# A decode-attention kernel: the value step turned round (keys' values stream past fixed probabilities) and the branch sum spread over four column groups

## The chip, the cores and the metric

The kernel runs on one core of one Trainium2 chip. The metric is device time in microseconds (us), the median over several executions of the same program. Two executions of this kernel are rarely more than 0.4% apart (192.45 to 193.17 us over eight).

In the text, PE is the matrix engine (TensorE), PEld its weight loads, DVE the vector engine, ACT the scalar engine, POOL GpSimd and SP the engine that issues most transfers. A matmul has a fixed operand, loaded as weights, and a moving operand, which streams past it column by column. "Granted clock" is the share of PE's full clock that the chip's throttle let through, as the profile shows it.

## The reference, cut to what matters

One token for each of two batch rows goes through attention over a cached window of 4096 keys, beside a dense branch; both are added to the input.

```python
# B=2, Sq=1, D=448; 16 query heads, 8 key/value heads (rep=2), head size 256
W = min(4096, max(256, Sk // 4))                  # 4096
q = (xn @ wq) split into 16 heads of 256
k = k_cache[:, :, Sk - W:, :]; v = v_cache[:, :, Sk - W:, :]   # each kv head serves 2 query heads
scores = einsum("bhqd,bhkd->bhqk", q, k) * 256 ** -0.5
p = softmax(scores)
o = einsum("bhqk,bhkd->bhqd", p, v)
attention = o.reshape(B, 1, 16 * 256) @ wo        # 4096 -> 448
h = xn @ w1 + b1                                  # 448 -> 1792
dense = (h * tanh(softplus(h))) @ w2              # 1792 -> 448
out = x + attention + dense                       # (2, 1, 448), bf16
```

All inputs are bf16. Keys and values are 2 MB per (key/value head, batch row), 16 such pairs of each, and with the weights some 78 MB have to be read.

## The kernel before, in words

The kernel works through 16 "heads" `i` (a key/value head and a batch row; `b = 1` at odd `i`). Everything is issued in the order written, on every engine (`issue_in_order`).

For each head there are two halves `s = 2i` and `2i + 1`, of 16 blocks of 128 keys each:

- `turn(s)` (L356): DVE transposes the half's keys in 32x32 blocks, once the 2 MB of keys have landed.
- `scores(s)` (L368): eight matmuls of 512 columns with the spread-out query (`qdiag`, built by POOL in `build_q`, L249) as weights. ACT takes the exponential (L378) and, with it, the row sums.
- `turn_p(s)` (L389): DVE transposes the probabilities. After the second half it forms the sums (L396, L399), PE adds them over partitions (`den`, L403), and DVE takes the reciprocal `rec` (L405).
- `values(i)` (L415): 64 matmuls. Each loads 128x128 of the values as weights and moves 2 columns (the two query heads' probabilities) past them. The result, 128 partitions x 2 halves of the head size x 2 query heads, lies in `po`, of which there are two in turn. DVE multiplies it by `rec` into `oT` (L426).
- `mix(kvh)` (L206, by the helper `add`): after each second head, eight matmuls with two columns of `oT` (both batch rows) as weights and 224 columns of `wo` moving, added into `psA`, one tile of two rows for each half of the 448 output columns.

The main loop (L457) goes over `i = 0..17`. In turn `i` it issues the loads of keys `i+2` and values `i`; then for each half `turn(s+1)`, `scores(s)`, `turn_p(s-1)`; and at the end `values(i-2)` and, at odd heads, `mix`. Turn 16 has only the last `turn_p`, `values(14)`; turn 17 `values(15)` and the last `mix`. At the end (L487, L488) DVE and ACT each copy one half of the sum to `res`, and SP sends it out.

All big loads go through SP's queue, in order: keys into four buffers, values into five (shared with `wq`, `w1`, `w2`), `wo` into three. So the load of values `i` waits for `values(i-5)` to be done with its buffer. The last head's values come in three pieces, and the last `wo` in two.

The dense branch is done in the first two turns: `dense_in` (L275) and `dense_out`, whose 28 matmuls go through `add` as well.

Of the kernel before, what the change touches and what calls it, by code (L numbers as in the profile page):

```python
# [9 lines left out]
ALU = mybir.AluOpType  # L10
AXIS = mybir.AxisListType
BF16 = mybir.dt.bfloat16
FP32 = mybir.dt.float32
PSUM = bass.MemoryType.PSUM
# [20 lines left out]
def kernel(  # L35
# [13 lines left out]
    nc = tc.nc  # L49
    P = 128  # L50
    Q = 32
    NQ = P // Q

    Bsz, Sq, D = A_x.shape
    _, Hkv, Sk, Dh = A_k_cache.shape
    HqDh = A_wq.shape[1]
    Hq = HqDh // Dh
    rep = Hq // Hkv
# [3 lines left out]
    T = W // P  # L62
    NH = 2
    TH = T // NH
# [6 lines left out]
    ND = Dh // P  # L71
    NB = Dh // (2 * Q)
    NE = 2
    assert Sq == 1 and D * NX == NS * P and NS % 2 == 1 and HF % P == 0 and Hq % NX == 0
    assert TH * Q <= 512 and NB * NE * Q == Dh and ND == 2
    scale = float(Dh) ** -0.5
# [3 lines left out]
    ident = lead.tile([P, P], BF16)  # L80
    hsel = lead.tile([P, Q], FP32)
# [4 lines left out]
    consts = ctx.enter_context(tc.tile_pool(name="consts", bufs=1))  # L86
    p_pool = ctx.enter_context(tc.tile_pool(name="pp", bufs=3))
    small = ctx.enter_context(tc.tile_pool(name="small", bufs=3))
    ps_sc = ctx.enter_context(tc.tile_pool(name="ps_sc", bufs=2, space=PSUM))
    ps_o = ctx.enter_context(tc.tile_pool(name="ps_o", bufs=2, space=PSUM))  # L90
    ps_den = ctx.enter_context(tc.tile_pool(name="ps_den", bufs=1, space=PSUM))
    ps_a = ctx.enter_context(tc.tile_pool(name="ps_a", bufs=1, space=PSUM))
    ps_m = ctx.enter_context(tc.tile_pool(name="ps_m", bufs=1, space=PSUM))
# [2 lines left out]
    x_bf = consts.tile([Bsz, D], BF16)  # L96
# [14 lines left out]
    for lo, hi in ((0, SC), (SC, NS)):  # L111
        w = v_tile((hi - lo) * HW).rearrange("p (s n) -> p s n", n=HW)
# [2 lines left out]


    make_identity(nc, ident[:])
    eps_t = consts.tile([Bsz, 1], FP32)
    nc.vector.memset(eps_t[:], 1e-5)

# [7 lines left out]
        out=rstd[:], in_=mv[:, 1:2], func=ACT.Sqrt, bias=eps_t[:], scale=1.0  # L128
# [5 lines left out]
    for r in range(2):  # L134
        n = (NS + 1 - r) // 2
        nc.vector.tensor_scalar(  # L136
            out=xn_bf[:, r : NS : 2, :, :],
            in0=bass.AP(
                x_all.tensor,
                x_all.offset,  # L140
                [list(x_all.ap[0]), [1, n], [NS, P // 2], [(NS + r) // 2, 2]],
            ),
# [7 lines left out]
    for b4 in range(NB):  # L150
        rows = slice(b4 * Q, (b4 + 1) * Q)
        for j in range(NQ):
            nc.vector.tensor_copy(
                out=spread[rows, b4, j * Q : (j + 1) * Q], in_=ident[rows, rows]
            )
    hsel = hsel[:, 0:rep]
    nc.vector.tensor_copy(out=hsel, in_=ident[:, 0:rep])
    for j in range(1, NQ):
        nc.vector.tensor_tensor(
            out=hsel, in0=hsel, in1=ident[:, j * Q : j * Q + rep], op=ALU.add  # L160
        )
    ones_f = consts.tile([P, P], FP32)
    nc.gpsimd.memset(ones_f[:], 1.0)
# [2 lines left out]
    for i in range(NW):  # L166
        t = consts.tile([P, NB * NE, P], BF16, name=f"qdiag{i}")
# [30 lines left out]
    nc.vector.memset(ones[:], 1.0)  # L198


    NO = 2
    DO = D // NO
    psA = [ps_a.tile([Bsz, DO], FP32, name=f"psA{n}") for n in range(NO)]

    def add(n, lhsT, rhs, **flags):
        nc.tensor.matmul(psA[n][:, :], lhsT=lhsT, rhs=rhs, skip_group_check=True, **flags)  # L206

    for n in range(NO):
        add(n, ident[0:Bsz, 0:Bsz], x_bf[:, n * DO : (n + 1) * DO], start=True, stop=False)


    qrep = consts.tile([P, NB, HH, NE, NX, Bsz], BF16)
# [28 lines left out]
    def build_q(i):  # L241
        kvh, b = heads[i]
        x, h0 = divmod(kvh * rep, HH)
        t = qdiag[i % NW]
        tv = t[:].rearrange("p (n e) c -> p n e c", e=NE)
        for j in range(NQ):
            rows = slice(j * Q, (j + 1) * Q)
            for e in range(NE):
                nc.gpsimd.tensor_copy(  # L249
                    out=tv[rows, :, e, j * Q : j * Q + rep],  # L250
                    in_=qrep[rows, :, h0 : h0 + rep, e, x, b],
                )

# [55 lines left out]
    def dense_out():  # L309
        w2_sb = dense.pop("w2")  # L310
        for x in range(NX):
            for c in range(NF):
                for n in range(NO):
                    add(
                        n,
                        act_bf[:, c, x, :],
                        w2_sb[:, x, c, n * DO : (n + 1) * DO],
                        start=False,
                        stop=False,
                    )  # L320


    NSTEP = len(heads) * NH
# [28 lines left out]
    def turn(s):  # L352
        kt = kt_pool.tile([P, TH * Dh], BF16, tag="kt", name="kt")
        i, half = divmod(s, NH)
        k = k_t[i] if half < NH - 1 else k_t.pop(i)
        nc.vector.transpose(  # L356
            out=kt[:].bitcast(FP32),
            in_=k[:, half * TH * Dh : (half + 1) * TH * Dh].bitcast(FP32),
        )
        kt_t[s] = kt  # L360
# [26 lines left out]
    def turn_p(s):  # L387
        pT = p_pool.tile([P, TH * Q], BF16, tag="pT", name="pT", bufs=7)
        nc.vector.transpose(out=pT[:], in_=p_t.pop(s)[:])  # L389
        pT_t[s] = pT  # L390
        i, half = divmod(s, NH)
        if half != NH - 1:
            return
        rs = state.pop(("rs", i))
        sums = small.tile([P, rep], FP32, tag="sums", name="sums")
        nc.vector.tensor_scalar(  # L396
            out=sums[:], in0=hsel, scalar1=rs[:, 0:1], scalar2=None, op0=ALU.mult
        )
        nc.vector.scalar_tensor_tensor(  # L399
            out=sums[:], in0=hsel, scalar=rs[:, 1:2], in1=sums[:], op0=ALU.mult, op1=ALU.add  # L400
        )
        den = ps_den.tile([P, rep], FP32, tag="den", name="den")
        nc.tensor.matmul(den[:], lhsT=ones_f[:], rhs=sums[:], start=True, stop=True)  # L403
        state["rec", i] = small.tile([P, rep], FP32, tag="rec", name="rec", bufs=4)
        nc.vector.reciprocal(out=state["rec", i][:], in_=den[:])  # L405

    def values(i):
        kvh, b = heads[i]
        po = ps_o.tile([P, ND, rep], FP32, tag="o", name="o")
        vv = v_t.pop(i).rearrange("p t (m c) -> p t c m", c=ND)  # L410
        for t in range(T):
            half, th = divmod(t, TH)
            pTv = pT_t[i * NH + half][:].rearrange("p (t c) -> p t c", t=TH)
            for c in range(ND):
                nc.tensor.matmul(  # L415
                    po[:, c, :],
                    lhsT=vv[:, t, c, :],
                    rhs=pTv[:, th, 0:rep],
                    start=(t == 0 and c == 0),
                    stop=(t == T - 1),  # L420
                    skip_group_check=True,
                )
        if b == 0:
            state["oT"] = small.tile([P, ND, rep, Bsz], BF16, tag="oT", name="oT")
        oT = state["oT"]
        nc.vector.tensor_tensor(  # L426
            out=oT[:, :, :, b],
            in0=po[:],
            in1=state.pop(("rec", i))[:].unsqueeze(1).to_broadcast([P, ND, rep]),
            op=ALU.mult,  # L430
        )

    def mix(kvh):
        oT = state["oT"]
        w = wo_t.pop(kvh)
        for h in range(rep):
            for n in range(NO):
                for c in range(ND):
                    add(
                        n,  # L440
                        oT[:, c, h, :],
                        w[:, h, c * D + n * DO : c * D + (n + 1) * DO],
                        start=False,
                        stop=(kvh == Hkv - 1 and h == rep - 1 and c == ND - 1),
                    )

    NK = len(heads)
    KA = 2
# [5 lines left out]
    build_q(0)  # L454
    build_q(1)
    turn(0)
    for i in range(NK + KA):  # L457
        if i + 2 < NK:
            load_k(i + 2)
        if i < NK:  # L460
            load_v(i, (0, T) if i < NK - 1 else (0, T // 2, 3 * T // 4, T))
            kvh, b = heads[i]
            if b == Bsz - 1:
                load_wo(kvh, parts=1 if i < NK - 1 else 2)
            for half in range(NH):
                s = i * NH + half
                if s + 1 < NSTEP:
                    turn(s + 1)
                scores(s)
                if s >= 1:  # L470
                    turn_p(s - 1)
            if i + 2 < NK:
                build_q(i + 2)
        if i == NK:
            turn_p(NSTEP - 1)
        if i == 0:
            dense_in()
        if i == 1:
            dense_out()
        if i >= KA:  # L480
            values(i - KA)
            kvh, b = heads[i - KA]
            if b == Bsz - 1:
                mix(kvh)

    res = consts.tile([Bsz, D], BF16)
    nc.vector.tensor_copy(out=res[:, 0:DO], in_=psA[0][:, :])  # L487
    nc.scalar.copy(out=res[:, DO:D], in_=psA[1][:, :])  # L488
    nc.sync.dma_start(out=out.flatten_outer_dims(), in_=res[:])
    issue_in_order(tc)  # L490


# [28 lines left out]
```

The softmax here doesn't subtract the row's maximum and nothing guards it: scores larger than these inputs give would overflow.

## Time and profile before

| what | value |
|---|---|
| median of 8 executions | 192.76 us (192.45 to 193.17) |
| the profiled execution, its own time | 192.9 us |
| its span, first to last instruction | 191.1 us |
| mean granted clock | 0.827 |
| PE busy, PEld busy | 130.0 us (68%), 75.7 us (40%) |
| DVE, ACT, POOL busy | 108.4 us (57%), 25.4 us (13%), 24.9 us (13%) |
| bytes moved, mean rate | 77.90 MB, 408 GB/s |
| DVE at L356, waiting for keys | 43.6 us idle |
| DVE at L389 (transposed probabilities) | 32 of 671 ns |
| ACT at L378 (128x512 from the accumulator memory) | 32 of 597 ns |
| DVE at L426 (128x4 from the accumulator memory) | 16 of 135 ns |

How to read it: "busy" is the time in which an engine had an instruction running, and an engine that waits is idle however late its work is. Times in the text such as "at 176.04" are microseconds from the start of the span. The profiled execution's time is 1.8 us more than its span (192.9 against 191.1); the rest lies ahead of the first and behind the last instruction.

### The profile page before, as it was taken

The page shows a single profiled execution, that of the slowest core. Times are in us where ns is not written, and L with a number is a line of the kernel's source. Part 1 is how long each engine was busy: PE and PEld are TensorE (multiplying, and loading weights), DVE is VectorE, ACT ScalarE, POOL GpSimd, SP SyncE. Part 2 cuts the span into 40 slices and gives each one's busy share as a digit, 9 for nine tenths or more (in the row PEclk, how much of TensorE's full clock was granted, in tenths as well). Part 3 has the DMA queues.
Part 4 walks back from the last instruction along what each step waited for, and adds up shares of the span by engine and source line. Part 5 has one row for each costly group of instructions (what it writes and reads, how often), then busy time and mean ns, then how long its engine had stood idle before and what let it go on. Part 6 is the DMA issues. An engine that isn't in the chain of part 4 may idle for free.

```text
span 191.1 us, 3752 instructions
## 1 busy us (share of the span) xinstructions
PE 130.0 (68%) x1592; PEld 75.7 (40%) x1592; DVE 108.4 (57%) x169; ACT 25.4 (13%) x69; POOL 24.9 (13%) x139
## 2 busy tenths in 40 slices
PE   0252992699657947397619863794649576977994
PEld 0151391265343525244414523362424424443582
DVE  4706406898739390929375764848192755748131
ACT  5000110112110211012200211021101111021100
POOL 8005220022020202002200202020200200000000
PEclk9999995699995899569975998589957958696665
DMA  6999999999999999999999999999999999999960
GB/s 227 419 446 409 434 436 432 432 413 421 435 429 436 436 422 418 436 425 419 438 429 436 420 435 425 425 429 422 432 436 432 411 450 418 422 420 437 412 250 2
DMA packets 7818, 77.90 MB, mean 408 GB/s; under 512 B 757, under 2 KB 2809, under 8 KB 3322
## 3 DMA queue, kind: packets, MB, share of 16 engines
q1 hardware_dynamic: 7796, 77.66, 96.1%
q8 instruction: 12, 0.20, 0.4%
q14 instruction: 4, 0.03, 0.0%
q10 hardware_dynamic: 6, 0.01, 0.0%
HBM read 77.67 MB, written 0.00 MB: 406 GB/s over the span
## 4 chain that ended last, share of the span: by engine, by line
DMA 83%; DVE 7%; PE 6%; SPq 1%; issue 0%; ACT 0%
DMA v<-in_A_v_cache_dram 34%; DMA k<-in_A_k_cache_dram 33%; DMA wo<-in_A_wo_dram 16%; DVE kt L356 5%; PE o L415 3%; PE sc L368 2%; DVE pT L389 1%; PE psA L206 1%; PE den L403 1%; SPq L113 0%; SPq L330 0%; SPq L260 0%; SPq L265 0%; DVE sums L399 0%; DVE oT L426 0%
## 5 line engine op out<-in xcount | busy, mean ns | idle before, releaser
L356 DVE STREAM_TRANSPOSE kt<-k 128x2048 f32<-128x2048 f32 x32 | 73.5, 2300 | 43.6 <-DMA k<-in_A_k_cache_dram 43.6
L368 PE MATMUL sc<-kt,qdiag 128*128 128x512 bf16 x256 | 77.9, 458 | 13.4 <-DVE kt L356 13.4
L368 PEld LDWEIGHTS <-qdiag 128*128 128x128 bf16 x256 | 27.2, 115 | 50.5 <-issue 28.5
L378 ACT ACTIVATE p<-sc 128x512 bf16<-128x512 f32 x32 | 19.1, 597 | 146.0 <-PE sc L368 142.1
L249 POOL COPY qdiag<-qrep 32x8 bf16<-32x8 bf16 x128 | 20.9, 185 | 123.8 <-PE sc L368 109.0
L415 PEld LDWEIGHTS <-v 128*128 128x128 bf16 x1024 | 28.1, 97 | 4.0 <-issue 1.1
L415 PE MATMUL o<-pT,v 128*128 128x2 bf16 x1024 | 27.9, 163 | 0.0
L206 PE MATMUL psA<-wo,oT 128*2 128x224 bf16 x64 | 12.5, 371 | 21.8 <-DVE oT L426 21.8
L389 DVE STREAM_TRANSPOSE pT<-p 128x512 bf16<-128x512 bf16 x32 | 21.5, 671 | 0.0
L206 PEld LDWEIGHTS <-oT 128*2 128x2 bf16 x64 | 6.5, 112 | 25.0 <-DVE oT L426 22.5
L403 PE MATMUL den<-sums,ones_f 128*128 128x2 f32 x32 | 5.9, 255 | 12.4 <-DVE sums L399 12.4
L403 PEld LDWEIGHTS den<-sums,ones_f 128*128 128x128 f32 x32 | 6.2, 220 | 20.0 <-DVE sums L399 18.2
L405 DVE RECIPROCAL rec<-den 128x2 f32<-128x2 f32 x16 | 2.7, 170 | 17.0 <-PE den L403 17.0
L220 PE MATMUL qT_ps<-xs,v 128*128 128x4 bf16 x112 | 3.3, 166 | 5.4 <-DMA v<-in_A_wq_dram 2.9
L426 DVE TENSOR_TENSOR oT<-o,rec 128x4 bf16<-128x4 f32 x16 | 2.2, 135 | 7.6 <-PE o L415 7.6
L378 ACT ACTIVATION_READ_ACCUMULATOR p<-sc 128x1 f32 x32 | 6.2, 194 | 0.0
L220 PEld LDWEIGHTS <-v 128*128 128x128 bf16 x112 | 3.1, 104 | 5.9 <-DMA v<-in_A_wq_dram 5.9
L174 PE MATMUL xnT_ps<-ident,xn_bf 2*128 2x2 bf16 x7 | 0.5, 166 | 5.2 <-DVE xn_bf L136 5.2
L399 DVE SCALAR_TENSOR_TENSOR sums<-hsel,rs,sums 128x2 f32<-128x2 f32 x16 | 3.5, 221 | 0.6
L229 DVE CAST qT<-qT_ps 128x64 bf16<-128x64 f32 x1 | 0.2, 224 | 6.3 <-PE qT_ps L220 6.3
L275 PE MATMUL hT_ps<-xs,v 128*128 128x4 bf16 x49 | 3.7, 195 | 0.0
L275 PEld LDWEIGHTS <-v 128*128 128x128 bf16 x49 | 3.2, 151 | 0.3
(43 smaller groups left out, 28.6 us busy)
## 6 DMA issues: line engine op xcount, KB each, us to landing
k<-in_A_k_cache_dram SPq DMA_DIRECT2D x16, 2048.0 KB, 32.0
v<-in_A_v_cache_dram SPq DMA_DIRECT2D x15, 2048.0 KB, 35.0
v<-in_B_w_dram SPq DMA_DIRECT2D x2, 1568.0 KB, 21.0
wo<-in_A_wo_dram SPq DMA_DIRECT2D x7, 448.0 KB, 32.0
v<-in_A_wq_dram SPq DMA_DIRECT2D x1, 2048.0 KB
v<-in_A_wq_dram SPq DMA_DIRECT2D x1, 1536.0 KB, 10.6
v<-in_A_v_cache_dram SPq DMA_DIRECT2D x1, 1024.0 KB, 29.2
v<-in_A_v_cache_dram SPq DMA_DIRECT2D x2, 512.0 KB, 27.5
```

The source lines that it names most:

```text
L206: nc.tensor.matmul(psA[n][:, :], lhsT=lhsT, rhs=rhs, skip_group_check=True, **flags)
L220: nc.tensor.matmul(qT_ps[:, hh, e, :], lhsT=wq_v[s][:, hh, e, :], rhs=xs[:, s, :, :].rearrange("p x b -> p (x b)"), start=(s == 0), stop=( ...
L249: nc.gpsimd.tensor_copy(out=tv[rows, :, e, j * Q : j * Q + rep], in_=qrep[rows, :, h0 : h0 + rep, e, x, b],)
L275: nc.tensor.matmul(hT_ps[:, c, :, :].rearrange("p x b -> p (x b)"), lhsT=w1_v[:, s, c, :], rhs=xs[:, s, :, :].rearrange("p x b -> p (x b)" ...
L356: nc.vector.transpose(out=kt[:].bitcast(FP32), in_=k[:, half * TH * Dh : (half + 1) * TH * Dh].bitcast(FP32),)
L368: nc.tensor.matmul(psc[:], lhsT=qdiag[i % NW][:, n * NE + e, :], rhs=ktv[:, n, e, :, :], start=(n == 0 and e == 0), stop=(n == NB - 1 and ...
L378: nc.scalar.activation(out=p_sb[:], in_=psc[:].rearrange("p t c -> p (t c)"), func=ACT.Exp, scale=scale, accum_out=state["rs", i][:, s % N ...
L389: nc.vector.transpose(out=pT[:], in_=p_t.pop(s)[:])
L399: nc.vector.scalar_tensor_tensor(out=sums[:], in0=hsel, scalar=rs[:, 1:2], in1=sums[:], op0=ALU.mult, op1=ALU.add)
L403: nc.tensor.matmul(den[:], lhsT=ones_f[:], rhs=sums[:], start=True, stop=True)
L405: nc.vector.reciprocal(out=state["rec", i][:], in_=den[:])
L415: nc.tensor.matmul(po[:, c, :], lhsT=vv[:, t, c, :], rhs=pTv[:, th, 0:rep], start=(t == 0 and c == 0), stop=(t == T - 1), skip_group_check ...
```

## The change

1. In `values`, for heads 0 to 13, the operands change places. The probabilities of two blocks of keys for two query heads (4 columns, 16 apart) are the weights, and the values of the two blocks (2 x 256 = 512 columns) move past them. There are 16 such matmuls for a head. Of the 4 x 512 result only the parts where a block meets its own probabilities are used.
2. So that it can be used, ACT copies the 4 x 512 result (fp32) to `o_sb`; `finish` turns it with four fp32 transposes on PE into `pq`, of which there is one buffer; DVE copies one half, adds the other, and multiplies by `rec` (`scale_o`). `finish` and `mix` are issued by `close(i)`, one turn later than `values(i)`: after the first half's `turn_p`. For the last turns `close(13)` comes in turn 16, after the last `turn_p` and ahead of head 14.
3. Heads 14 and 15 keep the old form (`values_fixed`), but their result lies in the one buffer of `pq`.
4. The branch sum `psA` is one tile of 128 partitions, with the four results (batch row x half of the output columns) in rows 0, 32, 64 and 96. `add` issues four matmuls where it issued two, one for each row, each with one column as weights, in its own group of 32 columns of PE's array. `psA` is set to zero first, and the end is one copy by DVE and one transfer of four rows.
5. The query heads' columns in `qdiag`, `hsel` and the probabilities stand 16 apart rather than side by side.

```diff
-    psA = [ps_a.tile([Bsz, DO], FP32, name=f"psA{n}") for n in range(NO)]
...
+    NO = NQ // Bsz
     DO = D // NO
+    psA = ps_a.tile([P, DO], FP32, name="psA")
+    def add(lhsT, w, start=False, stop=False):
+        for b in range(Bsz):
+            for n in range(NO):
+                row = (b * NO + n) * Q
+                nc.tensor.matmul(
+                    psA[row : row + 1, :],
+                    lhsT=lhsT[:, b : b + 1],
+                    rhs=w[:, n * DO : (n + 1) * DO],
+                    start=start,
+                    stop=stop,
+                    tile_position=(0, row),
+                    skip_group_check=True,
+                )
+    nc.vector.memset(psA[:], 0.0)
+    add(ident[0:Bsz, 0:Bsz], x_bf[:, :], start=True)
...
+    NP = 2
+    NR = NP * rep
     def values(i):
+        po = ps_o.tile([NR, NP * Dh], FP32, tag="o", name="o")
+        v = v_t.pop(i)
+        for u in range(T // NP):
+            half, uh = divmod(u, TH // NP)
+            nc.tensor.matmul(
+                po[:],
+                lhsT=pT_t[i * NH + half][:, uh * NP * Q : (uh + 1) * NP * Q : HS],
+                rhs=v[:, u * NP : (u + 1) * NP, :].rearrange("p t d -> p (t d)"),
+                start=(u == 0),
+                stop=(u == T // NP - 1),
+            )
+        o_sb = small.tile([NR, NP * Dh], FP32, tag="o_sb", name="o_sb", bufs=1)
+        nc.scalar.copy(out=o_sb[:], in_=po[:])
+        state["o", i] = o_sb
...
+    def finish(i):
+        ov = state.pop(("o", i))[:].rearrange("r (u m c) -> r u c m", u=NP, c=ND)
+        pq = ps_q.tile([P, NP * ND * NR], FP32, tag="q", name="q")
+        pqv = pq[:].rearrange("p (u c r) -> p u c r", u=NP, c=ND)
+        for u in range(NP):
+            for c in range(ND):
+                nc.tensor.transpose(pqv[:, u, c, :], ov[:, u, c, :], ident_f[0:NR, 0:NR])
+        o = small.tile([P, ND, rep], FP32, tag="osum", name="osum")
+        nc.vector.tensor_copy(out=o[:], in_=pqv[:, 0, :, 0:rep])
+        for u in range(1, NP):
+            nc.vector.tensor_tensor(
+                out=o[:], in0=o[:], in1=pqv[:, u, :, u * rep : (u + 1) * rep], op=ALU.add
+            )
+        scale_o(i, o[:])
...
+    NFIX = 2
+    def close(i):
+        if i < NK - NFIX:
+            finish(i)
+        kvh, b = heads[i]
+        if b == Bsz - 1:
+            mix(kvh)
...
                 if s >= 1:
                     turn_p(s - 1)
+                if half == 0 and i > KA:
+                    close(i - KA - 1)
...
         if i == NK:
             turn_p(NSTEP - 1)
+            close(i - KA - 1)
...
         if i >= KA:
-            values(i - KA)
-            kvh, b = heads[i - KA]
-            if b == Bsz - 1:
-                mix(kvh)
+            if i - KA < NK - NFIX:
+                values(i - KA)
+            else:
+                values_fixed(i - KA)
+        if i >= NK:
+            close(i - KA)
-    res = consts.tile([Bsz, D], BF16)
-    nc.vector.tensor_copy(out=res[:, 0:DO], in_=psA[0][:, :])
-    nc.scalar.copy(out=res[:, DO:D], in_=psA[1][:, :])
-    nc.sync.dma_start(out=out.flatten_outer_dims(), in_=res[:])
+    res = consts.tile([P, DO], BF16)
+    nc.vector.tensor_copy(out=res[:], in_=psA[:])
+    nc.sync.dma_start(
+        out=out.rearrange("b s (n d) -> (b s n) d", n=NO), in_=res[0 : P : Q, :]
+    )
```

`values_fixed` is the old loop of 64 matmuls, into the first columns of a `pq` tile, followed by `scale_o`, the old multiplication at L426.

More of the change, by code (lines that the diff above doesn't have):

```diff
@@ L73 @@
     NE = 2
+    HS = Q // rep
     assert Sq == 1 and D * NX == NS * P and NS % 2 == 1 and HF % P == 0 and Hq % NX == 0
@@ L90 @@
     ps_o = ctx.enter_context(tc.tile_pool(name="ps_o", bufs=2, space=PSUM))
+    ps_q = ctx.enter_context(tc.tile_pool(name="ps_q", bufs=1, space=PSUM))
     ps_den = ctx.enter_context(tc.tile_pool(name="ps_den", bufs=1, space=PSUM))
@@ L117 @@
     make_identity(nc, ident[:])
+    ident_f = consts.tile([Q, Q], FP32)
+    nc.vector.tensor_copy(out=ident_f[:], in_=ident[0:Q, 0:Q])
     eps_t = consts.tile([Bsz, 1], FP32)
@@ L156 @@
     hsel = hsel[:, 0:rep]
-    nc.vector.tensor_copy(out=hsel, in_=ident[:, 0:rep])
+    nc.vector.tensor_copy(out=hsel, in_=ident[:, 0:Q:HS])
     for j in range(1, NQ):
         nc.vector.tensor_tensor(
-            out=hsel, in0=hsel, in1=ident[:, j * Q : j * Q + rep], op=ALU.add
+            out=hsel, in0=hsel, in1=ident[:, j * Q : (j + 1) * Q : HS], op=ALU.add
         )
@@ L198 @@
     nc.vector.memset(ones[:], 1.0)
-    NO = 2
+    NO = NQ // Bsz
     DO = D // NO
-    psA = [ps_a.tile([Bsz, DO], FP32, name=f"psA{n}") for n in range(NO)]
[L205 to L209, printed above, removed]
+    psA = ps_a.tile([P, DO], FP32, name="psA")
[14 more added lines that the diff above has]
+    add(ident[0:Bsz, 0:Bsz], x_bf[:, :], start=True)
     qrep = consts.tile([P, NB, HH, NE, NX, Bsz], BF16)
@@ L249, in build_q @@
                 nc.gpsimd.tensor_copy(
-                    out=tv[rows, :, e, j * Q : j * Q + rep],
+                    out=tv[rows, :, e, j * Q : (j + 1) * Q : HS],
                     in_=qrep[rows, :, h0 : h0 + rep, e, x, b],
@@ L312, in dense_out @@
             for c in range(NF):
[L313 to L320, printed above, removed]
+                add(act_bf[:, c, x, :], w2_sb[:, x, c, :])
     NSTEP = len(heads) * NH
@@ L405, in turn_p, with scale_o, values_fixed @@
         nc.vector.reciprocal(out=state["rec", i][:], in_=den[:])
+    NP = 2
+    NR = NP * rep
     def values(i):
-        kvh, b = heads[i]
-        po = ps_o.tile([P, ND, rep], FP32, tag="o", name="o")
+        po = ps_o.tile([NR, NP * Dh], FP32, tag="o", name="o")
[12 more added lines that the diff above has]
+        state["o", i] = o_sb
+    def scale_o(i, o):
+        kvh, b = heads[i]
+        if b == 0:
+            state["oT"] = small.tile([P, ND, rep, Bsz], BF16, tag="oT", name="oT")
+        nc.vector.tensor_tensor(
+            out=state["oT"][:, :, :, b],
+            in0=o,
+            in1=state.pop(("rec", i))[:].unsqueeze(1).to_broadcast([P, ND, rep]),
+            op=ALU.mult,
+        )
[9 more added lines that the diff above has]
+        for u in range(1, NP):
+            nc.vector.tensor_tensor(
+                out=o[:], in0=o[:], in1=pqv[:, u, :, u * rep : (u + 1) * rep], op=ALU.add
+            )
+        scale_o(i, o[:])
+    def values_fixed(i):
+        pq = ps_q.tile([P, NP * ND * NR], FP32, tag="q", name="q")
+        po = pq[:, 0 : ND * rep].rearrange("p (c h) -> p c h", c=ND)
         vv = v_t.pop(i).rearrange("p t (m c) -> p t c m", c=ND)
@@ L417, in values @@
                     lhsT=vv[:, t, c, :],
-                    rhs=pTv[:, th, 0:rep],
+                    rhs=pTv[:, th, 0:Q:HS],
                     start=(t == 0 and c == 0),
@@ L422, in values @@
                 )
[L423 to L431, printed above, removed]
+        scale_o(i, po)
     def mix(kvh):
@@ L436, in mix @@
         for h in range(rep):
[L437 to L445, printed above, removed]
+            for c in range(ND):
+                add(
+                    oT[:, c, h, :],
+                    w[:, h, c * D : (c + 1) * D],
+                    stop=(kvh == Hkv - 1 and h == rep - 1 and c == ND - 1),
+                )
     NK = len(heads)
@@ L480 @@
         if i >= KA:
-            values(i - KA)
-            kvh, b = heads[i - KA]
-            if b == Bsz - 1:
-                mix(kvh)
-    res = consts.tile([Bsz, D], BF16)
-    nc.vector.tensor_copy(out=res[:, 0:DO], in_=psA[0][:, :])
-    nc.scalar.copy(out=res[:, DO:D], in_=psA[1][:, :])
-    nc.sync.dma_start(out=out.flatten_outer_dims(), in_=res[:])
+            if i - KA < NK - NFIX:
[8 more added lines that the diff above has]
+        out=out.rearrange("b s (n d) -> (b s n) d", n=NO), in_=res[0 : P : Q, :]
+    )
     issue_in_order(tc)
```

## The prediction

> **What bounds the kernel now.** I began with the page's slices over time and its chain of work.
>
> ```profile
> PEclk9999995699995899569975998589957958696665
> DMA  6999999999999999999999999999999999999960
> ...
> DMA 83%; DVE 7%; PE 6%; SPq 1%; issue 0%; ACT 0%
> ```
>
> The transfer engines are full from the second slice to the last but one, and 83% of the chain is transfers. PE's clock goes up and down. What PE, DVE and ACT save in the middle is therefore worth nothing; what they need there costs nothing while it fits into the time in which a head's data arrives. Keys of successive heads start their transposes at 149.08, 159.86 and 169.86, so that is 10 to 11 us. Next, the chain in order of time, for its end:
>
> ```profile
> 133.32 36.52 DMA k<-in_A_k_cache_dram
> ...
> 169.86 2.31 DVE kt L356
> ...
> 176.04 0.58 PE den L403 x2
> 176.63 3.37 PE sc L368 x8
> 180.00 1.59 PE o L415 x64
> ...
> 183.20 3.42 PE o L415 x128
> 186.62 0.02 issue
> 186.64 0.17 DVE oT L426
> 186.81 0.04 issue
> 186.86 1.67 PE psA L206 x8
> 188.52 0.02 issue
> 188.55 0.33 ACT res L488
> ```
>
> The last keys land at 169.86. DVE turns them and the probabilities of head 14 until its sums are ready at 176.04. From there to 188.9 it is PE that sets the end, in the order in which it is written. This tail of 12.9 us is where the change acts. Third, how fast PE is in it: its busy time and clock in stretches of 3.41 us, the grid on which the clock is seen to change.
>
> ```profile
> 108.16:111.57 3.41, 2.13 (x18) 1.00 0.99 409
> 114.98:118.40 3.42, 1.51 (x61) 0.99 1.04 446
> 118.40:121.81 3.41, 1.35 (x8) 0.50 0.98 418
> 172.90:176.31 3.41, 2.66 (x9) 0.51 1.03 435
> 183.15:186.56 3.41, 3.41 (x129) 0.51 0.42 163
> ```
>
> The columns are PE's busy time, matmuls, clock, DMA share and rate. The state changes at the end of a stretch, by what was done in it. After 1.9 us of 512-column matmuls (first line, scores alone) the clock stays full; after a stretch with the old values only (second line, 61 matmuls) it is halved in the next. The last stretch begins halved and stays so, with PE busy all through on two-column matmuls. So the old values do not hold the clock up.
>
> **Prices.** Eight scores matmuls move PE on by 1.74 us at full clock (from 104.91 to the values at 106.65) and by about 3.4 at half (176.49 to 179.84): 217 and 425 ns each. The old values take 1.74 us at either clock (from 168.89 at full, and two heads in 3.54 from 183.06 at half). The 224-column matmuls follow each other in 99 ns at full clock (28 from 39.93 to 42.70) and in 198 at half (8 from 162.87 to 164.45).
>
> **The change, part by part.**
>
> *Values turned round, 14 heads.* Out go 64 x 27 ns = 1.74 us; in come 16 x 217 = 3.48 us at full clock, 6.8 at half. The moving operand has the scores' shape; loading 4 columns of weights should hide as the 2-column loads at L206 do. So each head costs PE +1.74 us.
>
> *Fold.* ACT copies 4 x 512: taken like the exponential of 512 elements, 0.60 us. Four fp32 transposes are not in the trace. Lower bound, the six two-row bf16 transposes at L174: 0.31/6 = 0.05 us each, 0.2 together. Upper, the fp32 `den` pair, 0.24 us at full clock (112.77 to 113.01), taken for each one: 1.0. I take one fp32 weight load of 128 columns each, 4 x 0.19 (median of L403) = 0.75, nearest in type and width. Three small DVE operations like L426 (0.135), with hand-overs: 0.55 us.
>
> *Column groups.* A `mix` goes from 8 matmuls to 16 of the same 224 columns. If four run side by side, 4 x 99 = 0.4 us at full clock; one after the other 16 x 99 = 1.58; at half clock 0.8 to 3.2. I take 0.8 for the sixth `mix` (warm) and 1.2 for the last (cold, as its cold 1.65 now), nearer to running together because the output rows lie apart. [...]
>
> *Middle, heads 0 to 13.* Per head PE needs warm 2 x 1.74 + 3.48 + 0.25 (`den`) + 0.75 + half of (0.55 + 0.8) = 8.6 us, below 10 to 11. In order behind the new values stand the next scores, behind the transposes the `mix`. `close` stands after the first half, so that ACT's copy is long done there. PE has to catch up with what the start leaves over: keys of head 4 make DVE wait at 55.72 now, and with 3.5 instead of 1.74 us for the first values PE gets there some 4 us later, then gains 1 to 2 us a head. All this is covered by the transfers. Later `values` free buffers later, on which SP's load waits; that wait is 0.4 us in all now:
>
> ```profile
> SPq L340 <- PE o L415: 0.4, 1, 0.4
> ```
>
> But keys issued at 133.32 land at 169.86, which at 408 GB/s is seven loads of 2 MB (5.1 us each) under way; SP may be some 25 us later (five of them) before the transfer engines run dry. The cost is 0.
>
> *Small edits.* The zeroing of `psA`, the fp32 identity, doubled `dense_out` (56 matmuls, 1.4 to 5.5 us for 2.8, before PE's slack at 55), POOL's 16-column stride (POOL is 13% busy): 0, hidden by transfers; DVE's start has 2.9 us of waiting for `wq` ahead of PE at 11.82. One 0.38 copy at the end for the overlapping pair: +0.05. The output as four rows instead of two: 0, between ±0.2 for want of a row.
>
> *Tail, warm.* From 176.04: `den` 0.25, transposes of head 12 0.75, scores 1.74 (3.35 cold now), values of 13 3.48: 182.26. ACT's copy with hand-over 0.7, in which `den` of 15 is hidden: 182.95. Transposes 0.75, DVE 0.55: 184.25. `mix` 0.8: 185.05. Values of 14, held until the fold has read the one `pq`: 1.84, DVE 0.25: 187.15. Values of 15 are now held by that same buffer (they followed at once): 1.84, 0.25: 189.25. Last `mix` 1.2: 190.45, copy 0.43: 190.9, against 188.9: **+2.0**.
>
> *Clock ahead of the tail.* In the middle PE has a light stretch of about 3.1 us in a turn (end of first scores, wait for DVE's sums, `den`, transposes). Where it falls into one 3.41 stretch, less than 1 us of long matmuls remains there, and the clock halves (1.08 us in 179.73 to 183.15 did not hold it, 1.66 did elsewhere). From the grid that happens in some two turns of three if PE is on time. It takes one full busy stretch to come back, so 3.4 to 6.8 us run at half speed: 1.7 to 3.4 us lost. If that is in turn 14, less the 0.7 us that PE would otherwise wait before 176.04, the tail starts 1.0 to 2.7 late. I take 0.9, the middle between none and 1.85. The sum is 2.0 + 0.9 = **+2.9**, a span of 194.0 and a time of 192.9 + 2.9 = 195.8. The profiled execution stood 0.14 over the median, so the median should be **195.7**. [...]
>
> **Rivals.**
>
> *No loss after all (0.20).* Scores warm save 1.6 us of the tail. If transposes cost 0.2, both `mix` 0.44 (16 starts at the 27 ns of L415), DVE's fold 0.45: 176.04 + 0.25 + 0.2 + 1.74 + 3.48 = 181.71, + 0.65 + 0.2 + 0.45 + 0.44 = 183.45, + two of 2.0 = 187.45, + 0.44 + 0.43 = 188.3, against 188.9: 0.6 faster, a median of 192.2. With one of these bounds missed it is about 192.7. For it: cold scores in the tail now. Against: every unknown at its low end. Half of this chance is faster. The decisive point is a fold plus two `mix` of together under 2.0 us.
>
> *The groups don't run together (0.12).* The change wouldn't do what it says: 1.58 + 3.17 for the two, 2.8 over my terms: 198.5. Also each middle `mix` keeps PE later.
>
> *PE cold at the end (0.06).* If the clock halves in turn 15, the last scores and values of 13 cost 1.6 + 3.3 more: over 200. Against it: on time, the light part there is only 1.7 us (175.35 to 177.04).
>
> **How the numbers follow.** The forecast (0.62) is 194.0 to 198.0 by its unknown terms. Within 0.2% cannot be told from no change here: 192.4 to 193.1. The range 192.6 to 199.3 leaves out half of the first rival and most of the last. Faster 0.10, same 0.10, slower 0.80.
>
> **What would show it.** The transfers' curve and the last keys' landing near 170 unchanged; 16 value matmuls near 217 ns; scores mostly at full clock; a gap on PE between values of 13 and the sixth `mix` of 2 us, and a small one between values of 14 and 15. Wrong if the last keys land over 0.5 us elsewhere, if PE has no idle time at all from turn 5 (then it bounds the middle), if the two `mix` take under 0.5 each, or if the clock in the last 20 us is lower than before.

## The result, and the profile after

| | before | after |
|---|---|---|
| median | 192.69 us (32 executions, 192.32 to 193.17) | 194.5 us (11 executions, 193.44 to 195.58) |
| profiled execution, time and span | 192.9, 191.1 us | 195.49, 193.7 us |
| mean granted clock, profiled | 0.827 | 0.891 |
| PE busy, instructions in all | 130.0 us, 3752 | 155.4 us, 2768 |

The ratio of the times is 1.0092 (95% interval 1.0076 to 1.0108): slower by 1.8 us, where 2.9 were forecast. The changed kernel's executions lie 2.1 us apart, before 0.9, and the profiled one is 1.0 over its median. Its spread belongs to the explanation.

The page of the changed kernel, its slices and its chain:

```profile
PEclk9999995869999699969997999859999999579965
DMA  6999999999999999999999999999999999999910
...
DMA 66%; PE 16%; DVE 14%; SPq 1%; issue 1%; ACT 0%; ACTq 0%
```

The clock is fuller than before, 0.891 in the mean against 0.827, and the transfer engines are as full as before up to the same place. But the chain has lost transfers to PE and DVE: 66% against 83%. Where PE comes in, the chain in order of time shows:

```profile
158.66 2.31 DVE kt L365
...
164.77 0.38 PE den L412 x2
165.15 0.58 PE q L453 x4
...
167.27 3.52 PE sc L377 x8
170.80 4.19 PE o L425 x16
174.99 1.85 PE sc L377 x8
176.84 0.12 PE den L412 x2
176.95 0.57 PE q L453 x4
177.52 1.85 PE sc L377 x8
179.37 3.56 PE o L425 x16
...
183.01 0.58 ACT o_sb L433
...
184.92 0.55 PE psA L214 x14
185.47 1.80 PE q L471 x64
...
187.51 1.84 PE q L471 x64
189.36 1.19 PE psA L214 x16
```

The last link to a transfer is the keys of head 14, at 158.66. The last keys, which before were on the chain at 169.86, are not on it at all: they land at 168.37, while PE is still at the second scores of head 14. From 166.36 to 182.93 PE is in work without a stop, and it is late because of two slow groups, scores at 167.27 (3.52 us) and values at 170.80 (4.19), where the same work takes 1.85 and 3.56 a few lines on. DVE's timeline shows by how much: the sums of head 14 are ready at 174.43, and DVE then waits 2.56 us for `den`, which PE begins at 176.68.

```profile
174.21 0.22 DVE L408 SCALAR_TENSOR_TENSOR sums<-hsel,rs,sums 128x2 f32<-128x2 f32 x1
176.99 0.17 DVE L414 RECIPROCAL rec<-den 128x2 f32<-128x2 f32 x1 [2.56 <-PE den L412]
```

The two profiled executions side by side (us):

| stretch | before | after | difference |
|---|---|---|---|
| to the last keys' landing | 169.86 | 168.37 | -1.49 |
| from there to `den` of head 14 | 6.18 | 8.31 | +2.13 |
| from there to the output's issue (188.91, 190.98) | 12.87 | 14.30 | +1.43 |
| from there to the end of the span | 2.19 | 2.72 | +0.53 |
| span | 191.1 | 193.7 | +2.6 |

The lines add up to the difference of these two executions, not to what each cause costs: an earlier landing is lost again where PE is late anyway. Each line of it was an object of the experiments.

### The profile page after: what moved, and what is told of

Same layout as the page of the kernel before. It is cut to its first block, busy times and chain, and to the rows that moved or that the text cites. A ratio compares the mean times of both kernels' runs of the same rounds, so it can differ in the third digit from the quotient of the medians.

```text
span 193.7 us, 2768 instructions
## 1 busy us (share of the span) xinstructions
PE 155.4 (80%) x1070; PEld 72.5 (37%) x1070; DVE 116.2 (60%) x199; ACT 33.1 (17%) x82; POOL 27.1 (14%) x139
## 4 chain that ended last, share of the span: by engine, by line
DMA 66%; PE 16%; DVE 14%; SPq 1%; issue 1%; ACT 0%; ACTq 0%
DMA k<-in_A_k_cache_dram 66%; DVE kt L365 9%; PE sc L377 6%; PE o L425 4%; PE psA L214 2%; DVE pT L398 2%; PE q L471 2%; PE q L453 1%; PE den L412 1%; SPq L115 0%; DVE sums L408 0%; ACT o_sb L433 0%; DVE oT L440 0%; SPq L276 0%; SPq L281 0%
## 5 line engine op out<-in xcount | busy, mean ns | idle before, releaser
L377 PE MATMUL sc<-kt,qdiag 128*128 128x512 bf16 x256 | 70.9, 425 | 9.0 <-DVE kt L365 7.9
L425 PE MATMUL o<-v,pT 128*4 128x512 bf16 x224 | 52.1, 386 | 0.0
L425 PEld LDWEIGHTS <-pT 128*4 128x4 bf16 x224 | 18.6, 88 | 33.2 <-issue 8.8
L433 ACT COPY o_sb<-o 4x512 f32<-4x512 f32 x14 | 8.0, 574 | 42.5 <-PE o L425 42.5
L214 PE MATMUL psA<-wo,oT 128*1 128x224 bf16 x128 | 9.0, 343 | 2.9 <-DVE oT L440 2.9
L453 PE MATMUL q<-ident_f,o_sb 4*128 4x4 f32 x56 | 8.9, 261 | 0.4 <-ACT o_sb L433 0.4
L453 PEld LDWEIGHTS q<-ident_f,o_sb 4*128 4x128 f32 x56 | 7.7, 206 | 0.7 <-ACT o_sb L433 0.5
L214 PEld LDWEIGHTS <-oT 128*1 128x1 bf16 x128 | 3.4, 93 | 5.4 <-DVE oT L440 4.7
L121 DVE CAST ident_f<-ident 32x32 f32<-32x32 bf16 x1 | 3.3, 3283 | 1.3 <-POOL ident masks.py:199 1.3
L471 PE MATMUL q<-pT,v 128*128 128x2 bf16 x128 | 3.7, 165 | 0.3 <-DVE oT L440 0.3
```

The lines of the kernel that those rows point to most:

```text
L121: nc.vector.tensor_copy(out=ident_f[:], in_=ident[0:Q, 0:Q])
L214: nc.tensor.matmul(psA[row : row + 1, :], lhsT=lhsT[:, b : b + 1], rhs=w[:, n * DO : (n + 1) * DO], start=start, stop=stop, tile_position= ...
L377: nc.tensor.matmul(psc[:], lhsT=qdiag[i % NW][:, n * NE + e, :], rhs=ktv[:, n, e, :, :], start=(n == 0 and e == 0), stop=(n == NB - 1 and ...
L425: nc.tensor.matmul(po[:], lhsT=pT_t[i * NH + half][:, uh * NP * Q : (uh + 1) * NP * Q : HS], rhs=v[:, u * NP : (u + 1) * NP, :].rearrange( ...
L433: nc.scalar.copy(out=o_sb[:], in_=po[:])
L453: nc.tensor.transpose(pqv[:, u, c, :], ov[:, u, c, :], ident_f[0:NR, 0:NR])
```

## The experiments

Times are medians of several executions with the kernel before run beside them on the same chip (192.60 to 192.74 us in these series). "The changed kernel" is 194.5.

**Head 13 in the old form as well.**

```diff
-    NFIX = 2
+    NFIX = 3
```

> Head 13 goes back to the old form too, so three heads keep it; the rest is the changed kernel. Theory (head 13's turned values and its fold are on the path in the tail): values 3.55 to 1.85 us, and copy, transposes and sums (183.0 to 184.9, with the denominators hidden under 0.3 of them) go, 3.2 us in all; PE then waits about 1.0 for the last sums, which DVE again forms after head 13's result. 2.2 us faster than the changed kernel: a median near 192.3. Rival (PE is simply too full in the middle, the tail only passes that on): 1.0 or less, the half head of work saved, 193.5 or more. Rival (the loss is in the column groups and the four-row output): 194.2 or more.

Measured: 192.53 us (ratio to before 0.9992, 0.9972 to 1.0012). That is 2.0 under the changed kernel, as the theory said, and too much for either rival. The executions spread from 191.3 to 193.9, and the profiled one (191.34) is among the fastest. PE's timeline:

```profile
177.45 1.79 PE L471 MATMUL q<-pT,v 128*128 128x2 bf16 x64
180.48 0.38 PE L412 MATMUL den<-sums,ones_f 128*128 128x2 f32 x2 [1.24 <-DVE sums L408]
180.79 0.55 PE L214 MATMUL psA<-wo,oT 128*1 128x224 bf16 x16
```

The values of 13 take 1.79 instead of 3.56, the fold behind them is gone, and PE waits 1.24 us for the last sums. One head's turned form in the tail is thus about the whole loss.

**Without the column groups.** One matmul of 448 columns for each piece, two rows, one copy and a two-row output.

```diff
-    psA = ps_a.tile([P, DO], FP32, name="psA")
+    psA = ps_a.tile([Bsz, D], FP32, name="psA")
...
+        nc.tensor.matmul(
+            psA[:, :], lhsT=lhsT, rhs=w, start=start, stop=stop, skip_group_check=True
+        )
```

> The branch sum goes back to two rows in one tile of 448 columns, one matmul for each piece instead of four in column groups, and the output to two rows; turned values and fold stay. Theory (groups run side by side and save a little, the four-row output costs a little): mix of head 13 four matmuls at 0.19 us, 0.8 instead of 0.48; the last at half clock 1.55 instead of 1.24; output 0.55 less. Together +0.1: 194.3 to 194.8. Rival (groups and switching cost more than they save): under 194.0.

Measured: 195.39 us (1.0139, 1.0103 to 1.0175), slower than the changed kernel by 0.9, with the intervals just overlapping. The rival fell, but the loss is larger than I expected. The `mix` at the end of this kernel and of the changed one, on PE:

```profile
185.98 1.84 PE L461 MATMUL q<-pT,v 128*128 128x2 bf16 x64 [0.26 <-DVE oT L430]
188.08 1.65 PE L211 MATMUL psA<-wo,oT 128*2 128x448 bf16 x4 [0.26 <-DVE oT L430]
```

```profile
187.51 1.84 PE L471 MATMUL q<-pT,v 128*128 128x2 bf16 x64 [0.26 <-DVE oT L440]
189.29 1.24 PE L214 MATMUL psA<-wo,oT 128*1 128x224 bf16 x16
```

Without groups the last `mix` waits 0.26 us for head 15's result and takes 1.65. With groups it takes 1.24 and begins before that result is there (DVE writes it at 189.39): its first matmuls have only the other batch row as weights. From `den` of head 14 to the output's issue the kernel without groups needs 15.71 us (174.70 to 190.41), the changed one 14.30; it has 0.53 back at the end. I had left out the earlier start and the wider copy (0.61 against 0.39).

**All heads in the old form, with the groups.** `NFIX = 16`.

> All sixteen heads keep the old form of the values; the column groups, the four-row output and the later place of mix stay. Theory (the groups save in the tail what the run without them lost, 0.9 us there of which half is that kernel's own wider copy at the end; the scores are cold again): last mix 1.24 instead of 1.65 us, mix of head 13 0.5 instead of 0.9, less 0.26 for the one buffer and 0.5 for the longer output: 192.2 to 192.7. Rival (the turned values, not the groups, make the last keys land near 168.6 instead of 169.86, or the groups alone are worth more): under 191.8. The landing of the last keys in the profile tells whether fewer PE instructions are behind the earlier landing: 169.9 if so, 168.6 if not.

Measured: 192.6 us (1.0006, 0.9993 to 1.0019). As expected, and with the last keys at 170.08. What the groups save in `mix` is here eaten by the longer output and by a wait for the last values (0.25 us, until 185.85), which the next run but one makes plain.

**PE's light stretch filled.** Four matmuls with no use after the first scores of a turn.

```diff
+        if s % NH == 0 and i > KA:
+            pd = ps_o.tile([P, TH, Q], FP32, tag="o", name="o")
+            for n in range(4):
+                nc.tensor.matmul(
+                    pd[:],
+                    lhsT=qdiag[i % NW][:, n * NE, :],
+                    rhs=ktv[:, n, 0, :, :],
+                    start=(n == 0),
+                    stop=(n == 3),
+                )
```

> The changed kernel with four matmuls of 512 columns added after the first scores of each turn from turn 3 on, where PE waits for DVE's sums; their result is not used. Theory (the light stretch lets the clock halve, and the cold stretch in turn 14 makes the tail late by 0 to 2.3 us depending on the grid): the work fits into a wait of 1.75 us, the clock holds, the lateness goes: a median of 193.4 to 193.9, and a spread below 1.0 us where the changed kernel has 2.1. Rival (PE is too full, whatever its clock): 0.87 us more a turn, a median of 195.0 or more.

Measured: 193.77 us (1.008, 1.0049 to 1.011): 0.7 less in the median for 0.87 us more work in each turn, as the theory said, and far from the rival's 195.0. But the interval overlaps that of the changed kernel (1.0076 to 1.0108), so the gain in time is not clear of noise; what the trace shows is the clock. The spread was not as expected: four executions lie at 193.6 to 193.8, two at 195.2 and 195.4, and these two have the lowest clocks (0.938 and 0.922 against 0.947 to 0.958). Stretches of the changed kernel around turn 14, PE's busy time, matmuls and clock, first for the whole engine, then for the scores alone:

```profile
161.76:165.17 3.41, 1.66 (x9) 1.00 1.03 435
165.17:168.59 3.42, 3.05 (x24) 0.51 1.03 441
168.59:172.00 3.41, 3.41 (x10) 0.50 0.94 392
```

```profile
161.76:165.17 3.41, 1.26 (x6) 1.00 1.03 435
```

The first stretch has 1.26 us of long matmuls (the rest of its 1.66 is `den`) and is followed by two at half clock. With the filler the same place reads

```profile
162.97 1.03 PE L387 MATMUL o<-kt,qdiag 128*128 128x512 bf16 x4
164.88 0.38 PE L422 MATMUL den<-sums,ones_f 128*128 128x2 f32 x2 [0.88 <-DVE sums L418]
...
166.96 1.91 PE L377 MATMUL sc<-kt,qdiag 128*128 128x512 bf16 x8
```

and the scores at 166.96 run at full clock. The traces of the other kernels with turned values bear on the spread. Where the profiled execution kept full clock in turn 14 (this kernel, three old heads, no column groups), it is among the faster ones of its kernel: 193.76, 191.34 and 194.4 us. Where the clock halved there (the changed kernel and, below, more instructions and the combined kernel), it is among the slowest: 195.49, 195.79 and 192.82. Two traces do not help: the run with two of four rows halved too, but its four executions lie within 0.5 us, and the run with six fillers is told below.

**The kernel before, filled likewise.** Eight matmuls with no use behind the values of heads 0 to 12.

```diff
+        if i < NK - 3:
+            pd = ps_o.tile([P, TH * Q], FP32, tag="o", name="o")
+            for n in range(8):
+                nc.tensor.matmul(
+                    pd[:],
+                    lhsT=qdiag[i % NW][:, n, :],
+                    rhs=pT_t[i * NH][:],
+                    start=(n == 0),
+                    stop=(n == 7),
+                )
```

> The kernel before with eight matmuls of 512 columns added behind the values of heads 0 to 12, where PE waits for keys; their result is not used. Theory (long matmuls hold the clock, so the last scores run at full clock, 1.9 instead of 3.35 us): 191.0 to 191.6 and a mean clock over 0.93. Rival (the clock in the tail does not matter, since DVE and transfers set the end): 192.4 to 192.9. Rival (added work on PE makes it late): 193.2 or more.

Measured: 192.67 us (0.9992, 0.9983 to 1.0), clock 0.907. My theory fell; the first rival's time came, and of its two reasons the transfers. PE's timeline:

```profile
176.34 1.90 PE L368 MATMUL sc<-kt,qdiag 128*128 128x512 bf16 x8
178.08 1.74 PE L415 MATMUL o<-pT,v 128*128 128x2 bf16 x64
...
183.31 1.01 PE L415 MATMUL o<-pT,v 128*128 128x2 bf16 x32 [0.26 <-DMA v<-in_A_v_cache_dram]
184.53 0.59 PE L415 MATMUL o<-pT,v 128*128 128x2 bf16 x16 [0.20 <-DMA v<-in_A_v_cache_dram]
185.79 0.58 PE L415 MATMUL o<-pT,v 128*128 128x2 bf16 x16 [0.67 <-DMA v<-in_A_v_cache_dram]
186.63 1.65 PE L206 MATMUL psA<-wo,oT 128*2 128x224 bf16 x8 [0.26 <-DVE oT L436]
```

The last scores are 1.6 us faster, as wanted, and PE then waits three times for pieces of the last values, until 185.79. Its last `mix` begins at 186.63; before, at 186.86. The old kernel's tail lay just over a floor that the transfers set, and this floor was not in my reading.

**More instructions.** Why do the last keys land earlier in the changed kernel? 64 two-column matmuls with no use in each of turns 3 to 10:

```diff
+        if s % NH == 0 and 3 <= i <= 10:
+            pd = ps_o.tile([P, 2], FP32, tag="o", name="o")
+            for n in range(64):
+                nc.tensor.matmul(
+                    pd[:],
+                    lhsT=qdiag[i % NW][:, n % 8, :],
+                    rhs=ktv[:, 0, 0, 0:2, 0],
...
```

> The changed kernel with 64 matmuls of two columns added in each of turns 3 to 10, after the first scores, where PE waits 1.75 us for DVE's sums; their result is not used, and they bring the instructions back to about the number of the kernel before (2768 plus 1024 against 3752). Theory (the last keys land 1.3 us earlier in the changed kernel because fewer instructions have to be fetched over the same transfer engines: 168.4 to 168.7 in six kernels with the turned values, 169.9 to 170.1 in three with the old): the last keys land at 169.6 to 170.2, the median is 195.2 to 196.0. Rival (the landing goes with the form of the values or with when buffers come free): 168.3 to 168.8, and 194.2 to 194.8.

Measured: 195.19 us (1.0135, 1.0113 to 1.0158), at the low end of what was expected, and the landing as expected. Against the changed kernel the median rose by 0.7 us, and the fastest execution by 1.3 (194.77 against 193.44). The queue that fetches instructions, with its packets, MB and share, in the changed kernel and in this one:

```profile
q8 instruction: 8, 0.13, 0.3%
```

```profile
q8 instruction: 12, 0.20, 0.4%
```

DVE's start on the last keys in the timeline, again the changed kernel first:

```profile
168.37 2.31 DVE L365 STREAM_TRANSPOSE kt<-k 128x2048 f32<-128x2048 f32 x1 [2.06 <-DMA k<-in_A_k_cache_dram]
```

```profile
169.81 2.31 DVE L365 STREAM_TRANSPOSE kt<-k 128x2048 f32<-128x2048 f32 x1 [2.07 <-DMA k<-in_A_k_cache_dram]
```

The kernel before has 12 packets and 169.86. All twelve traces fall into line: the last keys start at 168.37 to 168.70 in the eight kernels with 7 to 9 packets, and at 169.81 to 170.08 in the four with 12 or 13. This run alone leaves a rival, as its added work also makes DVE late in turns 3 to 10 (119.12 instead of 117.50) and some key loads are issued up to 0.8 us later. But the kernel before has no such delay and the same late landing, and the four and six fillers add work with few instructions and land at 168.54. So fewer instructions give the last keys 1.4 us. How so few packets do that is not shown. Between the kernel before and the changed one the landings agree to 0.3 us up to 138 us and part between 138 and 149; this run parts from the changed kernel between 128 and 139.

**The output's rows.** Two runs, each sending the first half of each output row only: from far partitions with the changed kernel's `psA`, and from neighbouring ones with the kernel without groups.

```diff
-        out=out.rearrange("b s (n d) -> (b s n) d", n=NO), in_=res[0 : P : Q, :]
+        out=out.rearrange("b s (n d) -> (b s) n d", n=NO)[:, 0, :], in_=res[0 : P : NO * Q, :]
```

> The changed kernel, but only the first half of each output row is sent (two rows of 448 bytes from two partitions instead of four from four); the second halves of the output are left out. Theory (the four-row output from four far partitions costs 0.3 to 0.55 us at the end: issue 0.65 instead of 0.33 us, span end 2.7 instead of 2.2 us behind the issue): 194.0 to 194.2. Rival (that difference is chance of one execution): 194.5 within 0.15.

Measured: 194.46 us (1.0093, 1.0079 to 1.0108), no change, which is the time that the rival gave. But the end is as long as in the changed kernel (2.65 us from the issue at 190.15 to the span's end at 192.8), so the long end isn't chance, and it doesn't come from the number of rows:

```profile
190.15 0.63 SPq L547 DMA_DIRECT2D out_dram<-res  x1
```

```diff
-    nc.sync.dma_start(out=out.flatten_outer_dims(), in_=res[:])
+    nc.sync.dma_start(out=out.flatten_outer_dims()[:, 0 : D // 2], in_=res[:, 0 : D // 2])
```

> The kernel without column groups, but only the first half of each of its two output rows is sent (two pieces of 448 bytes from neighbouring partitions instead of two of 896); the second halves of the output are left out. It tells whether the slower end of the changed kernel (issue 0.65 against 0.33 us, end 2.7 against 2.2 us behind the issue) comes from short pieces or from far partitions. Short pieces: 2.6 to 2.8 us from the issue to the end of the span. Far partitions: 2.1 to 2.3.

Measured, in a single execution: 2.18 us from the issue at 190.32 to the span's end at 192.5.

```profile
190.32 0.34 SPq L537 DMA_DIRECT2D out_dram<-res  x1
```

Short pieces are not it. The rows from partitions 32 or 64 apart cost the half microsecond.

**A version that beats both.** The changed kernel with three heads in the old form, the four fillers, two buffers for the folded result, and the last turn of the probabilities ahead of head 13's scaling.

```diff
+                po = values_fixed(i - KA)
+                if i == NK - 1:
+                    turn_p(NSTEP - 1)
+                scale_o(i - KA, po)
```

> The changed kernel with three heads in the old form, the four added matmuls in PE's light stretch, two buffers for the folded result (one for the turned one), and the last turn of the probabilities ahead of head 13's scaling. Theory: 192.5 of the kernel with three old heads, less 0.6 for the clock, 0.26 for the buffer, 0.8 for the last sums that no longer wait behind head 13: 190.7 to 191.3, under the kernel before. Rival (the tail is bound by the last transfers, not by PE): not below 192.3.

Measured: 191.17 us (0.9938, 0.9916 to 0.996), nine executions at 191.06 to 191.28 and three at 192.8. What each of the four edits brings was not tried one by one. With six fillers:

> The combined kernel with six added matmuls in the light stretch instead of four. The combined kernel's executions fall into two groups, nine near 191.15 and three near 192.8; the profiled one is of the latter and halves its clock in turn 14. Theory (the light stretch was just short of holding the clock when the grid lies badly): at least 90% of executions below 191.6, none above 192.3, median 191.0 to 191.3. Rival (the two groups have another cause, or added work only makes PE later): some executions near 192.8 again, or a median above 191.5.

Measured: 191.1 us (0.9918, 0.9905 to 0.9931). Five of seven executions are at 191.1 and two at 192.0 and 192.3, so the second group came nearer but did not go: the expectation on the spread was missed. The profiled execution (192.0) shows why for itself. The clock halved earlier, from 147.2 to 150.6, behind a stretch that the fillers just missed, with 0.89 us of 512-column matmuls and 0.81 us of column-group ones. With the later waits filled PE did not make up for it, and `den` of head 14 came 1.57 us after its sums (174.60 to 176.17). Whether the transfers set the 191.1 was not tried.

## Why the prediction was right, point by point

The time lay in the range and the direction was right; the increase was put 1.1 us too high. That it came so near is in part luck, as several terms were off on both sides: the tail after `den` was taken too long (2.0 for 1.43) and the landing came early, while the clock's loss and the output were taken too small.

- **Turned values, 3.48 us for 16.** Right: 3.55 to 3.56 warm, and the run with head 13 back in the old form confirms the place.
- **Fold.** Transposes 0.57 (0.75 taken, between the bounds 0.2 and 1.0), copy 0.58 (0.60), DVE 0.63 from the last transpose to the next `mix` (0.55). Right in sum.
- **Column groups.** They do run together: 16 matmuls pass in 0.55 us warm (at 180.79 with three old heads), where one after the other 1.58 were worked out. The sixth `mix` was over-sized by 0.3; the last, 1.2, was right. The rival in which they do not run together is out. The kernel is slower without the groups, 195.39 against 194.5 in the median. That one batch row's part starts early, 0.26 us, was not foreseen.
- **Clock ahead of the tail.** The mechanism was right: light stretch, half clock in turn 14, tail late. In the profiled execution `den` of head 14 comes 2.25 us after its sums (174.43 to 176.68), within the 1.0 to 2.7 given. That transposes leave a stretch light, as the 3.1 us assume, no run shows: here they lie almost wholly behind the stretch that let the clock halve (165.08 to 165.72, its end at 165.17). The 0.9 put in as the middle is too little for that execution; what the clock costs in the median is not shown, as only one execution of each kernel was profiled. That the spread of times goes with the clock fits it: the three fastest executions of the changed kernel have clocks of 0.904 to 0.913, the two slowest 0.891 and 0.892; it isn't strict, as one with 0.926 took 194.5.
- **The step that failed: the transfers' curve unchanged, at no cost and no gain.** "The last keys' landing near 170 unchanged" was wrong, and a landing over 0.5 us elsewhere was one of the prediction's own signs of being wrong. They landed 1.5 us earlier, and adding instructions took this back. With the late landing the changed kernel is 2.6 us slower than the kernel before (195.19 against 192.60), near the forecast 2.9; so the term left out was worth some 0.7 us of the median.
- **"From there to 188.9 it is PE that sets the end": only just.** The filled old kernel shows a floor of transfers close below. So the rival without a loss was mis-worked where it let warm scores pay 1.6 us: in the old form they pay nothing. With turned values they can pay, as the transfers end earlier: with three old heads the values of 15 run from 183.36 to 185.14 without a wait for a load, which in the filled old kernel went on until 185.79. The kernel with all heads in the old form and cheaper `mix` stays at 192.6.
- **Output as four rows, 0 with ±0.2.** Too small: +0.5, by the distance of the partitions.
- **Middle at no cost.** Right: bytes moved are the same to 0.1 MB at every 20 us, and the load waiting for a buffer behind the values (1.0 us in three waits now) starves nothing.
- **PE cold at the end.** Did not come in the profiled execution: the scores at 177.45 and values of 13 ran at full clock.

## What to carry to other kernels

An operand swap that trades small matmuls for a few long ones should be kept out of the tail, where only latency counts: three heads in the old form instead of two were worth 2.0 us. Before one engine is made faster at the end, work out the landing of the last transfer as a floor; a wait that shows no transfer can be 0.2 us above it (the last `mix` of the kernel before began at 186.86, that of the filled one, which waits for transfers, at 186.63). Count the instructions too: with 1024 more of them the last keys landed 1.4 us later.

## What the runs showed of the hardware that was not expected

- With long matmuls of no use added the clock was higher, 0.957 against 0.891 in the changed kernel's profiled execution and 0.907 against 0.827 in the old one's, and the kernel not slower: 193.8 us in the median against 194.5 for the changed one, with 0.87 us added in each turn, and 192.67 against 192.74 for the old one. The clock halved behind a stretch with 1.26 us of long matmuls, and in the filled old kernel it held behind one with 1.56 us of scores (111.12 to 114.53).
- Some 1000 more instructions, 0.07 MB of 77.9, went with the last keys landing 1.4 us later.
- An output from four partitions 32 apart took 0.5 us longer from the issue to the span's end than one from neighbouring partitions, for the same bytes (2.72 against 2.19 us, the changed kernel and the one without groups).
- At the start of the changed kernel DVE's conversion of the identity took 3.28 us and the statistics behind it 2.58 instead of 0.62; both ended at 4.62, just as POOL's clearing of `qdiag` ended (1.85 to 4.59):

```profile
1.34 3.28 DVE L121 CAST ident_f<-ident 32x32 f32<-32x32 bf16 x1 [1.34 <-POOL ident masks.py:199]
2.04 2.58 DVE L127 BATCH_NORM_STATS2 stats<-x_bf 2x6 f32<-2x448 bf16 x1
```

The kernel before has the same clearing at the same time but no such conversion, and its statistics were not held up, so it is the conversion that waited, and the statistics behind it:

```profile
2.13 0.62 DVE L123 BATCH_NORM_STATS2 stats<-x_bf 2x6 f32<-2x448 bf16 x1 [1.28 <-DMA x_bf<-in_A_x_dram]
```

What held the conversion until the clearing ended is not shown, as no run here took POOL's work away. PE's wait for `wq`, 1.4 us until 11.95, hid it.
